# FFN output projection of tiles 2 to 8 by Strassen's seven block products, block sums on VectorE and GpSimd

## The chip, the cores and the metric

The kernel runs on one core of one Trainium2 chip. That core has a matrix engine (TensorE: PE in the profile, and PEld for its weight loads), three engines for element-wise work (VectorE: DVE; ScalarE: ACT; GpSimd: POOL) and a queue engine (SyncE: SP). Engines run side by side and wait for each other on semaphores. The metric is device time of one execution in microseconds (us); lower is better. Before the change the median of 3 runs is 362.95 us (362.79 to 364.91).

## The reference

Causal attention in blocks of 64 keys, 8 batches, 8 heads, 576 positions, head size 64; its output, with the heads side by side, is the input `x` (4608 x 512) of a gated feed-forward layer:

```python
gate = np.maximum(x @ w_gate, 0.0)     # 4608 x 1536
val = x @ w_val                        # 4608 x 1536
return (gate * val @ w_out)            # 4608 x 512
```

Everything is given and returned in float32; the kernel's matrix products take bfloat16 and sum in float32.

## The kernel before, in words

**Tiles of the feed-forward layer.** `ffn_gen` walks over nine tiles of 512 tokens. Tiles 0 to 7 hold the first 512 positions of one batch each, tile 8 the last 64 positions of all eight batches. A tile has three parts. For each of twelve slices f of the 1536 hidden columns there are four matmuls for the gate and four for the value (`product`, line 663; the weights are the stationary operand, 512 tokens stream past). ACT applies the rectifier (`relu`, line 673) and DVE multiplies gate by value into a bf16 tile `hT` (`hidden`, line 679). Then the output projection (`out_mm`, line 748): four groups of 128 tokens, in each twelve matmuls of 512 columns, accumulated over f in one PSUM bank; after a group DVE copies the bank to an `ob` tile (`finish`, line 758) and a store on the ACT queue writes it out (`put`, line 647). In tile 8 the last group is cut into 352 and 160 columns, and its stores are divided between the ACT and SP queues (line 653).

**Attention beside it.** While tile j of the feed-forward layer runs, the attention of batch j + 1 is computed in four rounds per batch. A round first makes scores on PE (`visit`, line 450) into two PSUM pairs of banks, both of the pool `psum_sc` (named `sc`, two buffers of two banks), and two single banks (`one`, `ffnp`). ACT takes the exponentials in this order: the two single banks (line 462), the pair `first`, the pair `second` (line 455). Some 20 places later two sets of matmuls with v follow (line 585 and 599), which DVE divides by the sums (line 524). Tiles 7 and 8 have no attention beside them.

**What sets the order.** The order is written out by hand. Each step of the attention, of the loads and of the casts has a name and a place in the table `AT`; the place counts steps of `ffn_gen` (one `yield` is one matmul), 144 to a tile. `ffn(n)` lets that many steps of the feed-forward layer go first, then the named step is issued. In tiles 3 to 6 the fourth round's scores stand at 92 of 144, its third exponential at 98, its products with v at 112 and 116; the output projection begins at 96. In tile 2 the fourth round (`s15`) stands at 383.65, that is 0.35 before the output projection of that tile, which begins at 384. Each engine executes its own instructions in that order, and waits are derived from the tiles that an instruction reads and writes.

**Buffers.** `psum_ffn` has three single banks (`ffnp`) for gate, value, projection groups and some of the attention; `ob` has four buffers; `hT` thirteen; `stage` ten buffers of 4 KB, which hold loads in the first part of the kernel.

**GpSimd.** In the steady part POOL does nothing but issue the loads of the next batch: 11 of q and k (`l`, 9 places into the tile) and 6 of v (`lv`, 46 places in), line 338.

Of the kernel before, what the change touches and what calls it, by code (L numbers as in the profile page):

```python
# [10 lines left out]
FP = mybir.dt.float32  # L11
BF = mybir.dt.bfloat16
AX = mybir.AluOpType
# [4 lines left out]
def kernel(  # L18
# [10 lines left out]
    nc = tc.nc  # L29

    B, H, S, D = q.shape
# [5 lines left out]


    FIRST = 3
    BASE = {0: 0, 1: 512, 3: 896, 2: 1024}  # L40
    AW = 1600
    TW = 256
# [2 lines left out]
    sb = ctx.enter_context(tc.tile_pool(name="sb", bufs=1))  # L45
# [75 lines left out]
    class Early:  # L121
# [111 lines left out]
        def half(self, t, hg):  # L233
            return self.m[t][:, 1024 * hg : 1024 * hg + 1024].rearrange(
                "p (j n) -> p j n", j=4
            )
# [403 lines left out]
    store, late = [], []  # L640

    def put(j, s, ob, n0, n1):
        if j < B:
            r0 = S * j + 128 * s
            n = 64 if j == B - 1 and s < 3 else 128
            for i in range(0, 128, n):
                (nc.sync if i else nc.scalar).dma_start(
                    out[r0 + i : r0 + i + n, :], ob[i : i + n]
                )
        else:  # L650
            for i in range(2):
                r0 = S * (2 * s + i) + 512
                (nc.scalar, nc.sync)[i].dma_start(
                    out[r0 : r0 + 64, n0:n1], ob[64 * i : 64 * i + 64]
                )

    def ffn_gen():
        for j in range(B + 1):
            hT = []
            x = xT_of(j) if j < B else xTt.rearrange("p b h n -> p h b n")  # L660

            def product(to, t, c, f):
                nc.tensor.matmul(  # L663
                    to,
                    (wg, wv)[t][f // 4][:, c, 128 * (f % 4) : 128 * (f % 4) + 128],
                    x[:, c],
                    start=(c == 0),
                    stop=(c == 3),
                )

            def relu(gate):
                gate_sb = sb.tile([128, 512], BF, name="gate_sb", bufs=3)
                nc.scalar.activation(gate_sb, gate, AF.Relu)  # L673
                return gate_sb

            def hidden(gate_sb, val):
                h = sb.tile([128, 512], BF, name="hT", bufs=13)
                products.append(
                    nc.vector.tensor_tensor(out=h, in0=gate_sb, in1=val, op=AX.mult)  # L679
                )  # L680
                hT.append(h)

            first = 0
            if j < 2:
                first = 2
                acc = {
                    n: psum_ffn.tile([128, 512], FP, name="ffnp")
                    for n in ((0, 0), (0, 1), (1, 0))
                }
                for cs in ((0, 1), (2,)):  # L690
                    for t in range(2):
                        for f in range(2):
                            if (t, f) not in acc:
                                acc[t, f] = psum_sc.tile([128, 2, 512], FP, name="sc")[
                                    :, 0, :
                                ]
# [12 lines left out]
            pairs = []  # L709
            if j == 0:  # L710
                pairs = [(f, (range(4),)) for f in (2, 4, 6)] + [(8, ((0, 1), (2, 3)))]
                first = 10
            for f0, parts in pairs:
                acc = {
                    (t, f): psum_one.tile([128, 512], FP, name="one")
                    if (t, f) == (0, 0)
                    else psum_ffn.tile([128, 512], FP, name="ffnp")
                    for t in range(2)
                    for f in range(2)
                }  # L720
                gates = []
                for cs in parts:
                    for t in range(2):
                        for f in range(2):
                            for c in cs:
                                product(acc[t, f], t, c, f0 + f)
                                if c == 3 and t == 0:
                                    gates.append(relu(acc[t, f]))
                                if c == 3 and t == 1:
                                    hidden(gates[f], acc[t, f])  # L730
                                yield
            for f in range(first, 12):
                gate = (
                    psum_one.tile([128, 512], FP, name="one")
                    if (j, f) == (1, 2)
                    else psum_ffn.tile([128, 512], FP, name="ffnp")
                )
                val = psum_ffn.tile([128, 512], FP, name="ffnp")
                for t, c in [(t, c) for t in range(2) for c in range(4)]:
                    product((gate, val)[t], t, c, f)  # L740
                    if (t, c) == (0, 3):
                        gate_sb = relu(gate)
                    if (t, c) == (1, 3):
                        hidden(gate_sb, val)
                    yield

            def out_mm(op, s, f, n0, n1):
                nc.tensor.matmul(  # L748
                    op,
                    hT[f][:, 128 * s : 128 * (s + 1)],  # L750
                    wo[f // 4][:, f % 4, n0:n1],
                    start=(f == 0),
                    stop=(f == 11),
                )

            def finish(op, s, n0, n1):
                ob = sb.tile([128, 512], FP, name="ob", bufs=4)[:, 0 : n1 - n0]
                nc.vector.tensor_copy(ob, op)  # L758
                if store:
                    store.pop()()  # L760
                (store if j else late).append(lambda j=j: put(j, s, ob, n0, n1))

            groups = outs(j)
            while groups:
                some = 2 if j == 0 and len(groups) == 4 else 1
                ops = [
                    psum_ffn.tile([128, 512], FP, name="ffnp")[:, 0 : n1 - n0]
                    for _, n0, n1 in groups[:some]
                ]
                for f0 in (0, 4, 8) if some == 2 else (0,):  # L770
                    for op, (s, n0, n1) in zip(ops, groups):
                        for f in range(f0, f0 + 4 if some == 2 else 12):
                            out_mm(op, s, f, n0, n1)
                            if f == 11:
                                finish(op, s, n0, n1)
                            yield
                groups = groups[some:]
# [7 lines left out]
    def ffn(n):  # L785
        for _ in range(n):
            if next(gen, 0) == 0:
                return
# [19 lines left out]
    with tc.manual_schedule(engines={E.PE, E.DVE, E.Activation, E.Pool, E.SP}):  # L808
# [45 lines left out]
        place = [0]  # L854
# [419 lines left out]
        for b in range(4, B):  # L1274
            base = 144 * (b - 1)
            for i in range(4):
                r = 4 * b + i
                acts.update(round_at(r, ("dve", "one", "ffn", None)))
                for n, p in STEADY.items():
                    AT[f"{n}{r}"] = base + 30 * i + p  # L1280
            acts[f"L{b}"] = lambda b=b: last_keys(b)
            AT[f"L{b}"] = base + 11
            if b + 1 < B:
                acts[f"l{b + 1}"] = lambda b=b: load_qkv(b + 1, (0, 1), products[-1])
                acts[f"lv{b + 1}"] = lambda b=b: load_qkv(b + 1, (2,))
                acts[f"d{b + 1}"] = lambda b=b: dma_transposes(b + 1)
                for n, p in (("l", 9), ("lv", 46), ("d", 66)):
                    AT[f"{n}{b + 1}"] = base + p
        assert set(acts) == set(AT), set(acts) ^ set(AT)
        for n in sorted(acts, key=lambda n: AT[n]):  # L1290
            ffn(int(AT[n]) - place[0])
            place[0] = max(place[0], int(AT[n]))
            acts[n]()
        ffn(10**6)
        store.pop()()
# [28 lines left out]
```

## Time and profile before

| | |
|---|---|
| median of 3 runs | 362.95 us |
| lowest, highest | 362.79, 364.91 us |
| span of the profiled execution | 363.3 us |
| PE busy | 353.3 us, 97% of the span |
| DVE busy | 170.7 us, 47% |
| ACT busy | 167.9 us, 46% |
| POOL busy | 112.8 us, 31% |

No time of its own is listed for the profiled execution beside its span; the span is 0.35 us above the median of the runs. The page lists busy time by engine, the clock that was granted to TensorE by slice (nine tenths or more in all 40 slices here), a chain of waits that leads back from the last instruction, and groups of equal instructions with their count, total time, mean time, and the idle time of their engine just before them with what ended it. Matmuls overlap: the duration of one (379 ns for 512 columns) is longer than the distance from one to the next, so distances are read from starts.

### The profile page before, as it was taken

What the parts mean: (1) busy time and instruction counts of PE and PEld (TensorE: products, weight loads), DVE (VectorE), ACT (ScalarE), POOL (GpSimd) and SP (SyncE); (2) the same over time, 40 slices, a digit from 0 to 9 for tenths busy, and PEclk for the clock granted to TensorE, in tenths of its full rate; (3) what the DMA queues carried; (4) which work ended last, traced back from release to release, by engine and by line L of the source; (5) the groups of instructions that cost most, each with busy time, mean ns of one, the idle gap of its engine ahead of it and who ended that gap; (6) DMA issues with size and microseconds to landing.
All of it is one profiled execution on the core that took longest, in us unless ns stands there. A gap on an engine that the chain in (4) does not pass through costs nothing.

```text
span 363.3 us, 7423 instructions
## 1 busy us (share of the span) xinstructions
PE 353.3 (97%) x2933; PEld 176.9 (49%) x2933; DVE 170.7 (47%) x426; ACT 167.9 (46%) x265; POOL 112.8 (31%) x157
## 2 busy tenths in 40 slices
PE   7899999999998999999999999999999999999996
PEld 3544455545544555555555454554455544444443
DVE  4663456677433363444445443554255434333432
ACT  4933676696325850666055625553365403302310
POOL 4647645695209500680049001930000000000000
PEclk9999999999999999999999999999999999999999
DMA  8999999999999995899449951997220130031013
GB/s 245 298 357 374 314 239 255 189 156 138 186 203 108 141 154 137 56 146 186 109 49 145 169 133 46 130 157 152 81 16 14 54 102 0 0 88 29 1 41 105
DMA packets 152083, 49.97 MB, mean 138 GB/s; under 512 B 134512, under 2 KB 145008, under 8 KB 152048
## 3 DMA queue, kind: packets, MB, share of 16 engines
q0 software_dynamic: 70480, 8.85, 46.7%
q1 hardware_dynamic: 76480, 31.86, 44.8%
q10 hardware_dynamic: 5088, 8.78, 7.2%
q8 instruction: 23, 0.38, 0.5%
q14 instruction: 12, 0.10, 0.1%
HBM read 37.75 MB, written 9.44 MB: 130 GB/s over the span
## 4 chain that ended last, share of the span: by engine, by line
PE 89%; DMA 5%; ACT 4%; DVE 1%; issue 0%; POOL 0%; SPq 0%; POOLq 0%; DVEq 0%
PE ffnp L663 49%; PE ffnp L748 23%; PE sc L450 3%; PE ffnp L585 2%; PE one L450 2%; DMA xT<-xnat 2%; DMA stage<-in_moe_w_gate_dram 2%; PE one L585 2%; ACT attnT L414 2%; PE one L663 1%; ACT attnT L455 1%; PE ffnp L547 1%; PE one L794 1%; DMA kTt<-k_bt 1%; PE ffnp L599 1%; PE one L599 1%
## 5 line engine op out<-in xcount | busy, mean ns | idle before, releaser
L679 DVE TENSOR_TENSOR hT<-gate_sb,ffnp 128x512 bf16<-128x512 bf16 x106 | 72.6, 685 | 96.5 <-PE ffnp L663 70.7
L673 ACT ACTIVATE gate_sb<-ffnp 128x512 bf16<-128x512 f32 x103 | 62.1, 605 | 103.3 <-PE ffnp L663 93.6
L663 PE MATMUL ffnp<-xT,wv 128*128 128x512 bf16 x376 | 100.7, 379 | 0.0
L663 PE MATMUL ffnp<-xT,wg 128*128 128x512 bf16 x364 | 99.0, 379 | 1.1 <-DMA xT<-xnat 0.4
L748 PE MATMUL ffnp<-wo,hT 128*128 128x512 bf16 (+2 forms) x444 | 98.8, 373 | 0.0
L748 PEld LDWEIGHTS <-hT 128*128 128x128 bf16 x444 | 41.8, 98 | 45.5 <-issue 0.6
L663 PEld LDWEIGHTS <-wv 128*128 128x128 bf16 x432 | 40.1, 98 | 45.5 <-issue 3.2
L663 PEld LDWEIGHTS <-wg 128*128 128x128 bf16 x432 | 39.8, 98 | 44.6 <-issue 3.6
L455 ACT ACTIVATE attnT<-sc 128x1024 bf16<-128x1024 f32 x56 | 56.8, 1044 | 0.0
L758 DVE COPY ob<-ffnp 128x512 f32<-128x512 f32 (+2 forms) x37 | 25.0, 676 | 45.1 <-PE ffnp L748 44.7
L338 POOL DMA_DIRECT2D q_bf<-in_q_dram x20 | 17.8, 903 | 76.3 <-DVE hT L679 52.0
L462 ACT ACTIVATE attnT<-one 128x512 bf16<-128x512 f32 (+1 forms) x28 | 15.0, 536 | 53.8 <-PE ffnp L450 53.8
L585 PEld LDWEIGHTS <-attnT 128*128 128x128 bf16 x640 | 26.5, 97 | 13.9 <-DVE attnT L803 1.3
L338 POOL DMA_DIRECT2D v_bf<-in_v_dram x30 | 24.3, 853 | 6.8 <-PE one L585 2.2
L450 PEld LDWEIGHTS <-kTm 64*128 64x128 bf16 x384 | 11.3, 94 | 15.6 <-issue 7.8
L338 POOL DMA_DIRECT2D k_bf<-in_k_dram x20 | 17.7, 933 | 0.0
L450 PE MATMUL sc<-qTm,kTm 64*128 64x512 bf16 (+1 forms) x168 | 16.9, 305 | 0.0
L585 PE MATMUL ffnp<-v_bf,attnT 128*128 128x65 bf16 x320 | 15.0, 194 | 0.0
L462 ACT ACTIVATE attnT<-ffnp 128x512 bf16<-128x512 f32 (+1 forms) x28 | 15.0, 534 | 0.0
L803 DVE MEMSET attnT<- 64x128 uint32 x59 | 9.0, 165 | 12.0 <-ACT attnT L455 10.2
L524 DVE TENSOR_TENSOR xnat<-ffnp,recip 128x256 bf16<-128x256 f32 x32 | 13.6, 424 | 1.1
L585 PE MATMUL one<-v_bf,attnT 128*128 128x65 bf16 x250 | 11.6, 193 | 0.7 <-POOL v_bf L220 0.7
(122 smaller groups left out, 293.8 us busy)
## 6 DMA issues: line engine op xcount, KB each, us to landing
out_dram<-ob ACTq DMA_DIRECT2D x29, 256.0 KB, 2.4
stage<-in_moe_w_val_dram SPq DMA_DIRECT2D x6, 512.0 KB, 8.2
stage<-in_moe_w_gate_dram SPq DMA_DIRECT2D x6, 512.0 KB, 8.7
stage<-in_moe_w_out_dram SPq DMA_DIRECT2D x6, 512.0 KB, 10.5
q_bf<-in_q_dram POOLq DMA_DIRECT2D x20, 128.0 KB, 4.3
k_bf<-in_k_dram POOLq DMA_DIRECT2D x20, 128.0 KB, 5.8
v_bf<-in_v_dram POOLq DMA_DIRECT2D x20, 128.0 KB, 6.1
stage<-in_v_dram SPq DMA_DIRECT2D x19, 128.0 KB, 5.4
```

Source lines behind the costliest of these rows:

```text
L338: ins = nc.gpsimd.dma_start(dst, part_of)
L450: nc.tensor.matmul(o, kTm[b % 2][head_of(hh), c, hp, :], qT, start=True, stop=True)
L455: return lambda: nc.scalar.activation(at[:, :, lo : lo + 512], sc, AF.Exp, scale=scale)
L462: nc.scalar.activation(at[:, hh, 1024 : 1024 + w], third[hh][:, 0:w], AF.Exp, scale=scale)
L524: nc.vector.tensor_tensor(out=out, in0=av[:, 0:m, 0:64], in1=recip[:, 0:m].to_broadcast([rows, m, 64]), op=AX.mult,)
L585: nc.tensor.matmul(av[:, p, :], at[:, col : col + 128], v_bf[b % 2][:, c, h, :], start=(p == 0), stop=(c == p), skip_group_check=True,)
L663: nc.tensor.matmul(to, (wg, wv)[t][f // 4][:, c, 128 * (f % 4) : 128 * (f % 4) + 128], x[:, c], start=(c == 0), stop=(c == 3),)
L673: nc.scalar.activation(gate_sb, gate, AF.Relu)
L679: nc.vector.tensor_tensor(out=h, in0=gate_sb, in1=val, op=AX.mult)
L748: nc.tensor.matmul(op, hT[f][:, 128 * s : 128 * (s + 1)], wo[f // 4][:, f % 4, n0:n1], start=(f == 0), stop=(f == 11),)
L758: nc.vector.tensor_copy(ob, op)
L803: nc.vector.memset(o, 0.0)
```

## The change: seven block products

For tiles 2 to 8 the product of `h` (512 tokens x 1536) with `w_out` (1536 x 512) is no longer formed directly. The hidden columns are paired: pair c holds slices 2c and 2c + 1. With tokens, hidden columns and output columns halved, the product is a 2 x 2 block product, and Strassen's scheme forms it from seven block products instead of eight. Each of the seven has 256 tokens, 768 hidden columns and 256 output columns, that is twelve matmuls of 256 columns: 84 matmuls of 256 columns replace 48 of 512 (60 in tile 8).

- `weight_sums` (POOL, places 232 to 247) adds blocks of `w_out` once into three `stage` buffers; `weight_differences` (DVE, places 300 to 320) subtracts blocks in place in `wo`.
- `sums_of` makes, for each pair of each tile, two sums of blocks of `h` on DVE and one difference of blocks on POOL; six pairs in a tile. `hT` becomes seven buffers of a pair each.
- `seven_products` computes the products in the order 5, 2, 1, 3, 4, 6, 7. Products 5 and 2 go to `y` and `z`, the two banks of one `sc` pair; 1, 6 and 7 to `ffnp` banks; 3 is added onto `y`, 4 onto `z`. ACT copies out `y` after product 5, `y` after product 3 and `z` after product 4; DVE and POOL add and subtract them into the four output blocks, which are stored by `put_block`.
- A place table of 144 steps is mapped to 138 (`place_of`) from tile 2 on, since one `yield` now stands for two matmuls in the 42 steps of the projection.

```diff
+    SEVEN = 2
 ...
+    def weight_sums(c):
+        if c % 2 == 0:
+            sevens.append(sb.tile([128, 2048], BF, name="stage", bufs=10))
 ...
+        nc.gpsimd.tensor_tensor(
+            out=t[:, 0:256], in0=two[:, 0, 0:256], in1=two[:, 1, 256:512], op=AX.add
+        )
+        nc.gpsimd.tensor_tensor(
+            out=t[:, 256:768].rearrange("p (c n) -> p c n", c=2),
+            in0=two[:, :, 0:256],
+            in1=two[:, :, 256:512],
+            op=AX.add,
+        )
+    def weight_differences(c, eng):
+        two = wo[c // 2][:, 2 * (c % 2) : 2 * (c % 2) + 2, :]
+        for d, n in ((two[:, 0, 256:512], two[:, 1, 256:512]), (two[:, 1, 0:256], two[:, 0, 0:256])):
+            eng.tensor_tensor(out=d, in0=d, in1=n, op=AX.subtract)
+    def sums_of(h):
+        s = sb.tile([128, 2048], BF, name="stage", bufs=10)
+        nc.vector.tensor_tensor(
+            out=s[:, 0:512], in0=h[:, 0, :], in1=h[:, 1, :], op=AX.add
+        )
+        nc.vector.tensor_tensor(
+            out=s[:, 1024:1280], in0=h[:, 0, 0:256], in1=h[:, 1, 256:512], op=AX.add
+        )
+        nc.gpsimd.tensor_tensor(
+            out=s[:, 512:1024].rearrange("p (c n) -> p c n", c=2),
+            in0=h[:, :, 256:512],
+            in1=h[:, :, 0:256],
+            op=AX.subtract,
+        )
+        return s
+    def seven_products(j, pair, sums):
+        def times(to, which, p, c, first):
 ...
+            nc.tensor.matmul(
+                to,
+                left[:, 128 * p : 128 * p + 128],
+                right,
+                start=first,
+                stop=(c == 5),
+                skip_group_check=True,
+            )
 ...
+        def whole(to, which, new=True, cs=range(6)):
+            for p in range(2):
+                for c in cs:
+                    times(half(to, p), which, p, c, new and (p, c) == (0, 0))
+                    if c % 2:
+                        yield
+        def store_later(hi, n0, ob, p0=0, p1=2):
+            if store:
+                store.pop()()
+            store.append(lambda: put_block(j, hi, n0, ob, p0, p1))
+        yz = psum_sc.tile([128, 2, 512], FP, name="sc")
+        y, z = yz[:, 0, :], yz[:, 1, :]
+        for to, which in ((y, 5), (z, 2)):
+            yield from whole(to, which, cs=range(4))
+        for to, which in ((y, 5), (z, 2)):
+            yield from whole(to, which, new=False, cs=(4, 5))
+        g = sb.tile([128, 512], FP, name="ob", bufs=4)
+        nc.scalar.copy(g, y)
+        nc.vector.tensor_tensor(out=g, in0=z, in1=g, op=AX.add)
+        m1 = psum_ffn.tile([128, 512], FP, name="ffnp")
+        yield from whole(m1, 1)
+        nc.vector.tensor_tensor(out=g, in0=m1, in1=g, op=AX.subtract)
+        yield from whole(y, 3, new=False)
+        c12 = sb.tile([128, 512], FP, name="ob", bufs=4)
+        nc.scalar.copy(c12, y)
+        store_later(0, 256, c12)
+        c22 = sb.tile([128, 512], FP, name="ob", bufs=4)
+        nc.gpsimd.tensor_tensor(out=c22, in0=g, in1=c12, op=AX.add)
+        yield from whole(z, 4, new=False)
+        c21 = sb.tile([128, 512], FP, name="ob", bufs=4)
+        nc.scalar.copy(c21, z)
+        store_later(1, 0, c21)
+        nc.gpsimd.tensor_tensor(out=g, in0=g, in1=c21, op=AX.add)
+        m6 = psum_ffn.tile([128, 512], FP, name="ffnp")
+        yield from whole(m6, 6)
+        nc.vector.tensor_tensor(out=c22, in0=m6, in1=c22, op=AX.add)
+        store_later(1, 256, c22)
+        if j < B:
+            m7 = psum_ffn.tile([128, 512], FP, name="ffnp")
+            yield from whole(m7, 7)
+            nc.vector.tensor_tensor(out=g, in0=g, in1=m7, op=AX.subtract)
+            store_later(0, 0, g)
+        else:
+            for p in range(2):
 ...
+                nc.vector.tensor_tensor(
+                    out=half(g, p), in0=half(g, p), in1=m7, op=AX.subtract
+                )
+                store_later(0, 0, half(g, p), p, p + 1)
 ...
             def hidden(gate_sb, val):
-                h = sb.tile([128, 512], BF, name="hT", bufs=13)
+                if len(hT) % 2 == 0:
+                    pair.append(sb.tile([128, 2, 512], BF, name="hT", bufs=7))
+                h = pair[-1][:, len(hT) % 2, :]
 ...
+            def sum_pairs():
+                while j >= SEVEN and len(sums) < len(hT) // 2:
+                    sums.append(sums_of(pair[len(sums)]))
 ...
                     if (t, c) == (0, 3):
                         gate_sb = relu(gate)
+                        sum_pairs()
 ...
+            if j >= SEVEN:
+                sum_pairs()
+                yield from seven_products(j, pair, sums)
+                continue
 ...
+        for c in range(6):
+            AT[f"W{c}"] = 232 + 3 * c
+            AT[f"D{c}"] = 300 + 4 * c
+        def place_of(p):
+            j, o = divmod(p, 144)
+            if j < SEVEN:
+                return p
+            return 144 * SEVEN + 138 * (j - SEVEN) + min(o, 96) + max(0, o - 96) * 42 / 48
```

`put_block` writes a 256 x 256 block (two times 128 rows of 256 columns) in one store on the ACT queue for tiles 2 to 7; in tile 8 it writes 64 rows at a time, by turns on the ACT and SP queues, 16 stores where there were 10. `store_later` issues the store before the one that it is given, so the last block of a tile (`g`) is stored in the next tile, after the copy `c12`.

More of the change, by code (lines that the diff above doesn't have):

```diff
@@ L655, in put, with put_block @@
                 )
+    def put_block(j, hi, n0, ob, p0, p1):
+        n = slice(n0, n0 + 256)
+        rows = ob.rearrange("q (p n) -> q p n", n=256)
+        if j < B:
+            r0 = S * j + 256 * hi + 128 * p0
+            nc.scalar.dma_start(
+                out[r0 : r0 + 128 * (p1 - p0), n].rearrange("(p q) n -> q p n", q=128),
+                rows,
+            )
+        else:
+            for p in range(p0, p1):
+                for i in range(2):
+                    r0 = S * (4 * hi + 2 * p + i) + 512
+                    (nc.scalar, nc.sync)[i].dma_start(
+                        out[r0 : r0 + 64, n], rows[64 * i : 64 * i + 64, p - p0]
+                    )
@@ new lines @@
+    sevens = []
+    def weight_sums(c):
+        if c % 2 == 0:
+            sevens.append(sb.tile([128, 2048], BF, name="stage", bufs=10))
+        two = wo[c // 2][:, 2 * (c % 2) : 2 * (c % 2) + 2, :]
+        t = sevens[c // 2][:, 768 * (c % 2) : 768 * (c % 2) + 768]
+        nc.gpsimd.tensor_tensor(
[7 more added lines that the diff above has]
+        )
@@ new lines, in weight_differences @@
+    def weight_differences(c, eng):
+        two = wo[c // 2][:, 2 * (c % 2) : 2 * (c % 2) + 2, :]
+        for d, n in ((two[:, 0, 256:512], two[:, 1, 256:512]), (two[:, 1, 0:256], two[:, 0, 0:256])):
[15 more added lines that the diff above has]
+        return s
@@ new lines, in seven_products, with half @@
+    def seven_products(j, pair, sums):
+        def times(to, which, p, c, first):
+            two = wo[c // 2][:, 2 * (c % 2) : 2 * (c % 2) + 2, :]
+            t = sevens[c // 2][:, 768 * (c % 2) : 768 * (c % 2) + 768]
+            s, h = sums[c], pair[c]
+            left, right = {
+                5: (s[:, 0:256], two[:, 1, 256:512]),
+                2: (s[:, 256:512], two[:, 0, 0:256]),
+                1: (s[:, 1024:1280], t[:, 0:256]),
+                3: (h[:, 0, 0:256], two[:, 0, 256:512]),
+                4: (h[:, 1, 256:512], two[:, 1, 0:256]),
+                6: (s[:, 512:768], t[:, 256:512]),
+                7: (s[:, 768:1024], t[:, 512:768]),
+            }[which]
+            nc.tensor.matmul(
[5 more added lines that the diff above has]
+                skip_group_check=True,
+            )
+        def half(to, p):
+            return to[:, 256 * p : 256 * p + 256]
+        def whole(to, which, new=True, cs=range(6)):
[35 more added lines that the diff above has]
+        store_later(1, 256, c22)
+        if j < B:
+            m7 = psum_ffn.tile([128, 512], FP, name="ffnp")
+            yield from whole(m7, 7)
+            nc.vector.tensor_tensor(out=g, in0=g, in1=m7, op=AX.subtract)
+            store_later(0, 0, g)
+        else:
+            for p in range(2):
+                m7 = psum_ffn.tile([128, 512], FP, name="ffnp")[:, 0:256]
+                for c in range(6):
+                    times(m7, 7, p, c, c == 0)
+                    if c % 2:
+                        yield
+                nc.vector.tensor_tensor(
+                    out=half(g, p), in0=half(g, p), in1=m7, op=AX.subtract
+                )
+                store_later(0, 0, half(g, p), p, p + 1)
@@ L674, in relu @@
                 return gate_sb
+            pair = []
             def hidden(gate_sb, val):
-                h = sb.tile([128, 512], BF, name="hT", bufs=13)
+                if len(hT) % 2 == 0:
+                    pair.append(sb.tile([128, 2, 512], BF, name="hT", bufs=7))
+                h = pair[-1][:, len(hT) % 2, :]
                 products.append(
@@ L681, in hidden @@
                 hT.append(h)
+            sums = []
+            def sum_pairs():
+                while j >= SEVEN and len(sums) < len(hT) // 2:
+                    sums.append(sums_of(pair[len(sums)]))
             first = 0
@@ L1288 @@
                     AT[f"{n}{b + 1}"] = base + p
-        assert set(acts) == set(AT), set(acts) ^ set(AT)
+        acts.update({f"W{c}": lambda c=c: weight_sums(c) for c in range(6)})
+        acts.update(
+            {f"D{c}": lambda c=c: weight_differences(c, nc.vector) for c in range(6)}
+        )
+        for c in range(6):
+            AT[f"W{c}"] = 232 + 3 * c
+            AT[f"D{c}"] = 300 + 4 * c
+        assert set(acts) == set(AT), set(acts) ^ set(AT)
+        def place_of(p):
[3 more added lines that the diff above has]
+            return 144 * SEVEN + 138 * (j - SEVEN) + min(o, 96) + max(0, o - 96) * 42 / 48
         for n in sorted(acts, key=lambda n: AT[n]):
-            ffn(int(AT[n]) - place[0])
-            place[0] = max(place[0], int(AT[n]))
+            at = int(place_of(AT[n]))
+            ffn(at - place[0])
+            place[0] = max(place[0], at)
             acts[n]()
```

## The prediction

> **What bounds the kernel now.** I read the page first: which engine the chain of waits rests on, and at what clock.
>
> ```profile
> PEclk9999999999999999999999999999999999999999
> PE 89%; DMA 5%; ACT 4%; DVE 1%; issue 0%; POOL 0%; SPq 0%; POOLq 0%; DVEq 0%
> ```
>
> The chain is PE, at the full granted clock. Then the chain in order of time, at its end (start, length, engine, line, count):
>
> ```profile
> 318.24 10.36 PE ffnp L748 x48
> 328.60 20.72 PE ffnp L663 x96
> 349.32 10.40 PE ffnp L748 x60
> 359.74 0.33 DVE ob L758
> ```
>
> PE issues without a gap, so a matmul less is time less, and any wait of PE is time more. 48 matmuls of 512 columns take 10.36 us, 215.8 ns each. For narrower ones I take the timeline of the last groups: each copy starts when its group ends.
>
> ```profile
> 357.12 0.69 DVE L758 COPY ob<-ffnp 128x512 f32<-128x512 f32 x1 [1.90 <-PE ffnp L748]
> 358.91 0.53 DVE L758 COPY ob<-ffnp 128x352 f32<-128x352 f32 x1 [1.10 <-PE ffnp L748]
> 359.74 0.33 DVE L758 COPY ob<-ffnp 128x160 f32<-128x160 f32 x1 [0.31 <-PE ffnp L748]
> ```
>
> Twelve matmuls of 352 columns took 358.91 - 357.12 = 1.79 us, 149 ns each; twelve of 160 took 0.83 us, 69 ns each, every one with its own weight load. A straight line through these three is 0.417 ns a column plus 2.5 ns; 256 columns lie inside it: **109.2 ns**.
>
> **1. The matmuls.** A tile now takes 84 x 109.2 ns = 9.17 us instead of 10.36 (tile 8: 10.36 by 36 x 215.8 + 1790 + 830 = 10.39): 6 x 1.19 + 1.22 = **8.4 us less**. A slope error of 2% moves this by 1.3.
>
> The row for this is 215.8, 149 and 69 ns by width. The Trainium skill (TensorE: Matmul & The Clock Gate, Back-to-back issue gap) speaks against narrow matmuls: a sustained stream with weight loads costs about 131 ns at 512 columns and 81 at 128. Interpolated, about 98 ns at 256, an estimate from that page, 84 of them would take 8.2 us against 6.3 for 48, and the sum would be 13 us of loss in place of the 8.4 of gain. The trace disagrees at 512 columns (215.8), so I stay with the rows.
>
> **2. The first product waits for an exponential.** `yz` is a pair of the two-buffer pool `sc`. By the order and waits of the built program, it takes the buffer of the fourth round's `first` pair, so product 5 waits for ACT's first exponential of that pair (ahead of it on ACT: relu and two exponentials). Before, out_mm used another pool and passed it. Timeline around the start of tile 4's projection, then tile 2's:
>
> ```profile
> 207.87 0.60 ACT L673 ACTIVATE gate_sb<-ffnp 128x512 bf16<-128x512 f32 x1 [1.59 <-PE ffnp L663]
> 208.36 0.59 ACT L462 ACTIVATE attnT<-one 128x512 bf16<-128x512 f32 x1
> 208.84 0.60 ACT L462 ACTIVATE attnT<-ffnp 128x512 bf16<-128x512 f32 x1
> 209.31 1.96 ACT L455 ACTIVATE attnT<-sc 128x1024 bf16<-128x1024 f32 x2
> 209.40 2.97 PE L748 MATMUL ffnp<-wo,hT 128*128 128x512 bf16 x13
> ```
>
> ```profile
> 132.73 4.48 PE L748 MATMUL ffnp<-wo,hT 128*128 128x512 bf16 x20
> 133.14 1.95 ACT L455 ACTIVATE attnT<-sc 128x1024 bf16<-128x1024 f32 x2
> ```
>
> L455 takes 1.04 us, so `first` is read at 209.31 + 1.04 = 210.35, with 0.07 for the release 210.42: PE, ready at 209.40, waits 1.02. Tiles 3, 5 and 6 show the same spacing. In tile 2 the round stands three matmuls nearer: 133.14 + 1.04 + 0.07 - 132.73 = 1.52. Everything of PE queues behind it. 4 x 1.02 + 1.52 = **5.6 us more**. Tiles 7 and 8 have no round there.
>
> **3. Product 4 waits for the copy of product 3.** `y` and `z` are two banks of one tile, and the built program makes product 4's first matmul (into `z`) wait for ACT's copy of `y`, which waits for product 3's last matmul. Nothing stands between the two on PE. Its price by rows of the same shape (PSUM to SBUF, 128 x 512):
>
> ```profile
> 329.30 1.03 PE L663 MATMUL ffnp<-xTt,wv 128*128 128x512 bf16 x4
> 329.56 0.60 ACT L673 ACTIVATE gate_sb<-ffnp 128x512 bf16<-128x512 f32 x1 [11.55 <-PE ffnp L663]
> ```
>
> ACT starts 0.26 us after PE has issued the last matmul (the next starts at 329.30), takes 0.60, release 0.07: 0.93. Seven tiles: **6.5 us more** (5.6 to 7.4 with copies of 0.48 to 0.73).
>
> **4. Product 3 waits for `z + g`** for the same reason: copy of `y`, then DVE. From the end of products 5 and 2: 0.26 + 0.60 + 0.06 + 0.69 + 0.07 = 1.68. In between PE has product 1, 12 x 0.109 = 1.31, and in tiles 2 to 6 two sets of products with v (0.45 each), which cover it. Tiles 7 and 8: 2 x 0.37 = **0.7 more**.
>
> **5. The rest of the chain to the next tile.** After product 3's end (t = 0): ACT's copy `c12` ends at 0.86; then the store of the previous tile's `g` is issued, and the copy `c21` needs that store's buffer, so ACT waits for its landing, 2.4 us by the page (2.0 to 3.3 in single windows): 3.3, copied 3.9. POOL adds 128 x 512 in f32. No such addition is in the trace; the one-input rows are
>
> ```profile
> L382 POOL CAST wo<-stage 128x1024 bf16<-128x1024 f32 x5 | 5.0, 1040 | 3.7 <-DMA stage<-in_moe_w_out_dram 3.7
> L195 POOL CAST q_bf<-stage 128x512 bf16<-128x512 f32 x5 | 3.1, 612 | 4.5 <-DMA stage<-in_q_dram 4.5
> ```
>
> between 0.61 (as many outputs) and 1.04 (as many elements read); no reason makes it free. I take 1.04 as nearer: 5.0. DVE's `g - m7` ends at 5.8 and frees the bank that the next tile's first value (or second gate) needs. PE gets there at 0.93 + 3 x 1.31 + 0.43 + 0.86 (scores) + 0.43 = 6.6: **covered by 0.8**, thanks to step 3. A landing of 3.3 would cost 0.1 a tile. Behind ACT's wait stand three stores (0.34 each, done at 5.0) and the next round's exponentials, whose scores come at 5.9; behind DVE's stands the next `hidden`, after 7. The Trainium skill (GPSIMD Reference, Engine selection) advises VectorE for additions, GpSimd being about twice as slow with two inputs; by its 4497 ns for 2048 f32 elements a quarter is 1.12 us, an estimate, and the sum stays.
>
> **6. The end.** Before: last matmul issued at about 359.48, the last copy ends 360.07, store lands 2.1 later, span ends 363.3. After, with t as above, PE ends at 4.9, `c21` at 3.9, POOL at 5.0, the two half subtractions (0.42 each, by L524) at 5.9. But the eight ACT stores of tile 8 stand behind `c21`; the 64-row stores took 0.5 us of queue each, and in the built program each waits for the landing of the store eight before it. That gives issue of c12, c21 from 3.95 to 5.95, c22 at 6.25 and 6.75 (landing of the first ones), `g` at 7.25 and 7.75, landing 9.85: 5.0 after PE's end against 2.7. **2.3 more**; 0.5 if the queue is no limit, 3.3 with landings of 2.7.
>
> **7. Covered work.** DVE: 12 sums a tile, 128 x 512 and 128 x 256 in bf16, at most 0.69 + 0.42 a pair by f32 rows, beside 2 x 0.69 of `hidden` in 3.45 us; 47% busy, and 0.77 us of slack before `hidden` holds a bank. The 12 differences at places 300 to 320 of tile 2 (0.17 by memset to 0.42 each) fill DVE nearly completely there: 0 to 2.5 us. POOL: 6 differences a tile, last needed by product 6; the sums of pairs 0 and 1 delay the v loads by up to 2.1 us, which are needed some 15 us later. The weight sums (12 in 9 us) end before place 300. On SP only 3 rows are fewer; transposes of xT keep their place. I take **0.5 more** for all this; 4 if DVE falls behind around rounds.
>
> **Sum**, against the execution's own span: 363.3 - 8.4 + 5.6 + 6.5 + 0.7 + 2.3 + 0.5 = 370.5. That span is 0.35 above the runs' median: **370.2 us**, 2% slower.
>
> **Rivals.**
> - *The handovers of the pair are cheap* (ends faster). Steps 2 to 4 are 12.8 us; without them 357.4. For: the copies are short and ACT is 46% busy. Against: the copy of step 3 starts only when product 3 has ended, and PE has nothing else. It is faster once the three cost under 7.2 in all, by 1% under 3.6.
> - *DVE and POOL fall behind*: two-input operations beside each other, sums at 0.69 + 0.42 and more, tile 2's differences: 4 to 8 us more, 374 to 378. For: DVE has stretches of six tenths. Against: its mean.
> - *256 columns do not cost half*: at 120 ns a matmul 6.4 us more, 376.6. Against: 69 ns at 160.
> - *Little change*: handovers at half, end at 0.5: 362 to 364.
>
> **How the numbers follow.** Forecast (366.6 to 373.5) 0.70; DVE/POOL 0.13; costly matmuls 0.04; little change 0.09; cheap handovers 0.04. The range leaves out the last two and the far end: **366.5 to 377**. One per cent, 3.6 us, is about what a measurement tells from no change: faster 0.04, same 0.10, slower 0.86.
>
> **What would show it.** PE idle before the products' line: about 1.0 us in each of tiles 3 to 6 and 1.5 in tile 2 released by an ACT exponential, 0.9 in all seven by an ACT copy, 0.4 in two by DVE; starts 109 ns apart within a product; the last store landing about 5 us after the last matmul. I am wrong if PE passes from product 3 to 4 without a gap, or if DVE and POOL rows grow so that PE waits elsewhere.

## The result: 4.3% slower

| | before | after |
|---|---|---|
| median | 362.87 us (4 runs) | **378.79 us** (378.19 to 379.38, 4 runs) |
| ratio | | **1.043** (95%: 1.039 to 1.046) |
| span of the profiled execution | 363.3 us | 377.5 us |
| PE busy | 353.3 us | 349.4 us |
| DVE busy | 170.7 us | 228.7 us |
| POOL busy | 112.8 us | 194.4 us |

The forecast was 370.2 us, the range 366.5 to 377: right that it gets slower, 8.6 us too low, and the range ends 1.8 short. In all later profiles the span lies 1.8 to 2.0 below the time of its execution. By that, before's profile (363.3) is of an execution of about 365.1 (an estimate), some 2 above its median, and not 0.35 as the prediction had it. Its base is unharmed, since it carried a difference of 7.2 over to the median; but the spans differ by 14.2 and the medians by 15.9, and a difference of spans of these two kernels is good to 2 us only.

### The profile page after: what moved, and what is told of

Its sections match the earlier page's. It is cut to its first block, busy times and chain, and to the rows that moved or that the text cites. A ratio compares the mean times of both kernels' runs of the same rounds, so it can differ in the third digit from the quotient of the medians.

```text
span 377.5 us, 8089 instructions
## 1 busy us (share of the span) xinstructions
PE 349.4 (93%) x3173; PEld 201.4 (53%) x3173; DVE 228.7 (61%) x522; ACT 180.0 (48%) x286; POOL 194.4 (51%) x225
## 5 line engine op out<-in xcount | busy, mean ns | idle before, releaser
L834 DVE TENSOR_TENSOR hT<-gate_sb,ffnp 128x512 bf16<-128x512 bf16 x106 | 72.4, 683 | 64.7 <-PE ffnp L814 40.4
L814 PE MATMUL ffnp<-xT,wv 128*128 128x512 bf16 x376 | 100.7, 379 | 3.9 <-DVE hT L834 3.8
L814 PE MATMUL ffnp<-xT,wg 128*128 128x512 bf16 x364 | 99.0, 379 | 3.2 <-DVE hT L834 2.4
L709 POOL TENSOR_TENSOR stage<-hT 128x512 bf16<-128x512 bf16 x42 | 54.0, 1313 | 80.7 <-DVE hT L834 80.7
L814 PEld LDWEIGHTS <-wv 128*128 128x128 bf16 x432 | 40.1, 98 | 50.3 <-issue 8.9
L814 PEld LDWEIGHTS <-wg 128*128 128x128 bf16 x432 | 39.9, 98 | 46.0 <-issue 6.8
L740 PEld LDWEIGHTS <-stage 128*128 128x128 bf16 x420 | 40.4, 98 | 11.5 <-issue 6.1
L706 DVE TENSOR_TENSOR stage<-hT 128x256 bf16<-128x256 bf16 x42 | 31.9, 761 | 0.0
L703 DVE TENSOR_TENSOR stage<-hT 128x512 bf16<-128x512 bf16 x42 | 31.0, 739 | 1.2
L740 PE MATMUL ffnp<-stage 128*128 128x256 bf16 x252 | 31.3, 273 | 0.0
L781 POOL TENSOR_TENSOR ob<-ob 128x512 f32<-128x512 f32 x7 | 8.8, 1264 | 36.1 <-ACT ob L778 36.1
L740 PE MATMUL sc<-wo,hT 128*128 128x256 bf16 x168 | 20.6, 272 | 5.2 <-ACT ob L778 5.0
L740 PE MATMUL sc<-wo,stage 128*128 128x256 bf16 x168 | 19.5, 272 | 4.7 <-ACT attnT L456 4.7
L910 PE MATMUL ffnp<-wo,hT 128*128 128x512 bf16 x96 | 23.6, 379 | 0.0
L740 PEld LDWEIGHTS <-hT 128*128 128x128 bf16 x168 | 16.4, 97 | 8.7 <-issue 6.8
```

The source lines that it names most:

```text
L703: nc.vector.tensor_tensor(out=s[:, 0:512], in0=h[:, 0, :], in1=h[:, 1, :], op=AX.add)
L706: nc.vector.tensor_tensor(out=s[:, 1024:1280], in0=h[:, 0, 0:256], in1=h[:, 1, 256:512], op=AX.add)
L709: nc.gpsimd.tensor_tensor(out=s[:, 512:1024].rearrange("p (c n) -> p c n", c=2), in0=h[:, :, 256:512], in1=h[:, :, 0:256], op=AX.subtract,)
L740: nc.tensor.matmul(to, left[:, 128 * p : 128 * p + 128], right, start=first, stop=(c == 5), skip_group_check=True,)
L814: nc.tensor.matmul(to, (wg, wv)[t][f // 4][:, c, 128 * (f % 4) : 128 * (f % 4) + 128], x[:, c], start=(c == 0), stop=(c == 3),)
L910: nc.tensor.matmul(op, hT[f][:, 128 * s : 128 * (s + 1)], wo[f // 4][:, f % 4, n0:n1], start=(f == 0), stop=(f == 11),)
```

## The profile after

The granted clock and the chain of waits (page of the kernel after). The clock has not changed. The chain stops short: it follows the end back over a fifth of the span.

```profile
PEclk9999999999999999999999999999999999999999
PE 18%; ACT 1%; DVE 0%; issue 0%; ACTq 0%
```

The end of that chain in order of time (start, length, engine, line, count) shows tile 8's products 3, 4, 6 and 7:

```profile
365.68 1.49 PE sc L740 x12
...
367.23 0.59 ACT ob L778
...
367.87 1.47 PE sc L740 x12
369.33 2.63 PE ffnp L740 x24
```

Products 6 and 7 are 24 matmuls. The first starts at 369.17 (the chain counts it only from the end of the one before) and the last at 371.68: 109 ns from one to the next, as priced. Product 4 starts 2.19 after product 3 (367.87 - 365.68) instead of 1.31: 0.88 for the handover.

What PE waited for (engine, line waited for, us in total, times, longest):

```profile
PE ffnp L814 <- DVE hT L834: 6.2, 8, 1.2
PE sc L740 <- ACT ob L778: 5.0, 7, 0.7
PE sc L740 <- ACT attnT L456: 4.7, 5, 1.3
```

The second and third lines are steps 3 and 2. This list counts a wait from the modelled end of the matmul before, so by starts each wait is longer. Step 2 in tile 4:

```profile
214.83 1.04 PE L814 MATMUL ffnp<-xT,wv 128*128 128x512 bf16 x4
...
215.62 1.96 ACT L456 ACTIVATE attnT<-sc 128x1024 bf16<-128x1024 f32 x2
...
216.72 2.45 PE L740 MATMUL sc<-wo,stage 128*128 128x256 bf16 x21 [0.84 <-ACT attnT L456]
```

The last of the four matmuls starts at 215.49, so the product could start 0.22 later, at 215.71. It starts at 216.72: a wait of 1.01, where the list has 0.84. Tiles 3, 5 and 6 show the same 1.01 and tile 2 shows 1.49, which makes 5.5 in all where the list has 4.7.

The first line is new. L814 is the feed-forward matmul, L834 `hidden`: PE waits for a bank that DVE has not yet read. The timeline of the longest of these waits, DVE, POOL and PE together:

```profile
241.09 0.69 DVE L834 TENSOR_TENSOR hT<-gate_sb,ffnp 128x512 bf16<-128x512 bf16 x1 [0.27 <-PE ffnp L814]
241.48 2.38 POOL L709 TENSOR_TENSOR stage<-hT 128x512 bf16<-128x512 bf16 x2
241.81 2.35 DVE L703 TENSOR_TENSOR stage<-hT 128x512 bf16<-128x512 bf16 x1
...
244.97 0.67 DVE L834 TENSOR_TENSOR hT<-gate_sb,ffnp 128x512 bf16<-128x512 bf16 x1
...
245.69 0.59 PE L814 MATMUL ffnp<-xT,wv 128*128 128x512 bf16 x2 [1.22 <-DVE hT L834]
```

One block sum of DVE (L703) takes 2.35 us. It ends 0.3 after the two differences on POOL beside it, as if it had to let both pass. `hidden` stands behind it in DVE's order, with some short operations of the attention between, and PE behind `hidden`. POOL had two differences to make in a row because its loads for the next batch stood before them. The `hidden` at 241.09 overlaps POOL too, and took 0.69 as ever; it reads one operand from PSUM, the sums read both from SBUF. Of 106 such operations in the trace none took more than 0.690.

By the starts of the stretches of PE, with the price per matmul confirmed, the 14.2 us of the spans divide so:

| stretch | before | after | difference |
|---|---|---|---|
| hidden part, tile 2 | 30.82 | 32.73 | +1.91 |
| tiles 3, 4, 5, 6 | 27.06 each | 30.16, 30.17, 30.57, 29.50 | +12.16 |
| tiles 7, 8 | 20.72 each | 20.72 each | 0 |
| projection, tiles 2 to 6 | 11.27 to 11.28 | 10.92 to 10.96 | -0.31 to -0.36 each |
| projection, tile 7 | 10.36 | 10.34 | -0.02 |
| tile 8's projection to the end | 14.17 | 16.06 | +1.90 |

The wait of step 2 ends at the products' first matmul, so its 5.5 is in the first two rows, which are 14.07 together: **8.5 us** of the hidden parts belong to no step of the sum, 8.1 of them in tiles 3 to 6. The 0.4 in tile 2 tells little: that stretch holds waits for loads and lies between 29.8 and 33.5 us in kernels that differ from this one in other places.

## Experiments

### DVE's sums beside POOL

One half of the sums is moved away, left out, or made lighter, in four ways. First the differences go to DVE:

```diff
-        nc.gpsimd.tensor_tensor(
+        nc.vector.tensor_tensor(
             out=s[:, 512:1024].rearrange("p (c n) -> p c n", c=2),
```

> The block differences of h (L709) go from POOL to DVE; nothing else moves. My theory now, A: DVE's sums L703 and L706 read two SBUF tiles and are held up for as long as a POOL operation with two SBUF inputs runs beside them; behind them stands hidden (L834), for which PE waits. By the stretches of the trace the cost is 9.2 us. So: L703 back to 0.42 and L706 to 0.28 each, no PE wait for L834, DVE's work on sums 42 x (0.42 + 0.28 + 0.42) = 47 us instead of 62.9, time 369 to 371. Rival B: DVE has simply too much to do, whoever is beside it; then 17.6 us more work on DVE makes PE wait longer for L834, 379 to 384. Rival C: POOL's queue is what holds (its loads for the next tile stand behind the differences); then the waits for L834 stay and those for loaded tiles go, 376 to 378.

Then POOL's half is left out (products 6 and 7 read `s[:, 0:256]` and `s[:, 256:512]`), and DVE's half (products 5, 2 and 1 read blocks of `h`):

> The block differences of h on POOL (L709) are left out; products 6 and 7 read the block sums in their place, so those two products are of other blocks. DVE's sums stay. A (two-input operations hold each other up): L703 0.42, L706 0.28, no PE wait for L834, 369 to 371. B (DVE's own load): 376 to 379, waits for L834 as before. Beside the kernel that has the differences on DVE it tells what these 42 operations cost there: nothing by A if DVE has the room.

> DVE's block sums of h (L703, L706) are left out; products 5, 2 and 1 read single blocks of h in their place. POOL's differences stay. A: the cost is in the pair, so leaving out this half takes it away as well: no PE wait for L834, L709 at 1.1 to 1.3 us, 369 to 371. C (POOL's queue alone): POOL's work and its loads stay as they are, so 376 to 379.

Last, POOL's operation keeps its size and loses its second input:

```diff
-        nc.gpsimd.tensor_tensor(
-            out=s[:, 512:1024].rearrange("p (c n) -> p c n", c=2),
-            in0=h[:, :, 256:512],
-            in1=h[:, :, 0:256],
-            op=AX.subtract,
+        nc.gpsimd.tensor_copy(
+            s[:, 512:1024].rearrange("p (c n) -> p c n", c=2), h[:, :, 256:512]
```

> POOL's 42 differences of h become copies of as many elements with one input (so products 6 and 7 are of single blocks); DVE's sums stay. It asks what of a POOL operation holds DVE's. If any POOL operation on SBUF does, for as long as it runs: POOL's copies take about 0.61 each instead of 1.31 (the one-input row of 128 x 512), a DVE sum is held up to 0.6, PE's waits for L834 shrink from 6.2 to 1 or 2, 371 to 374. If only a second input does: L703 0.42 and L706 0.28 in all rows, no such wait, 369 to 371.

| kernel | time, us | against after | L703 and L706, mean ns | PE waits for `hidden` |
|---|---|---|---|---|
| after | 378.79 | | 739, 761 | 6.2 us |
| differences on DVE | 371.45 (369.85 to 372.85) | -7.3 | 422, 283 | none listed |
| POOL's differences left out | 370.06 | -8.7 | 422, 283 | none listed |
| DVE's sums left out | 368.85 | -9.9 | left out | 0.3 us |
| POOL copies with one input | 369.83 | -9.0 | 538, 488 | none listed |

The last three rows are of 2 executions each. The kernel before took 362.7 to 363.6 us at the median beside the runs of this section, so a difference from the 378.79 is good to about 1 us.

The groups of the kernel after (count, then busy us and mean ns, then idle time before them):

```profile
L709 POOL TENSOR_TENSOR stage<-hT 128x512 bf16<-128x512 bf16 x42 | 54.0, 1313 | 80.7 <-DVE hT L834 80.7
L706 DVE TENSOR_TENSOR stage<-hT 128x256 bf16<-128x256 bf16 x42 | 31.9, 761 | 0.0
L703 DVE TENSOR_TENSOR stage<-hT 128x512 bf16<-128x512 bf16 x42 | 31.0, 739 | 1.2
```

With the differences on DVE:

```profile
L703 DVE TENSOR_TENSOR stage<-hT 128x512 bf16<-128x512 bf16 x42 | 17.7, 422 | 1.2
L709 DVE TENSOR_TENSOR stage<-hT 128x512 bf16<-128x512 bf16 x42 | 17.5, 417 | 0.0
L706 DVE TENSOR_TENSOR stage<-hT 128x256 bf16<-128x256 bf16 x42 | 11.9, 283 | 0.0
```

With one-input copies on POOL:

```profile
L709 POOL COPY stage<-hT 128x512 bf16<-128x512 bf16 x42 | 31.7, 788 | 90.7 <-DVE hT L831 90.7
L703 DVE TENSOR_TENSOR stage<-hT 128x512 bf16<-128x512 bf16 x42 | 22.6, 538 | 1.2
L706 DVE TENSOR_TENSOR stage<-hT 128x256 bf16<-128x256 bf16 x42 | 20.5, 488 | 0.0
```

The cost needs both halves: leave out either and it goes. In both runs that leave one out the hidden parts of tiles 3 to 6 are 28.07 us each, which is the 27.06 of before and the 1.01 of step 2, so nothing of the 8.1 us is left there. DVE makes all 126 operations in 47.1 us by itself, less than the 62.9 it took for 84 of them beside POOL. So DVE did not have too much to do, and rival B falls. The four times lie within 0.5 us of the 369 to 371 that theory A gave. Rival C, POOL's queue alone, falls with the run that leaves POOL's work as it is and DVE's sums out. With one input on POOL the sums are still held, by 13.5 us in all instead of 33.3, but PE no longer waits for `hidden`, which has that much room. Neither forecast for this run was right in full: the sums are held as by the first, the time is as by the second, and a copy took 0.79 us, not 0.61.

The Trainium skill states this (GPSIMD Engine Reference, Specifications): GpSimd shares its SBUF interfaces with VectorE, with contention where a VectorE instruction has two SBUF inputs or runs in a two-port mode. The trace agrees on both sides: the sums, two SBUF inputs, went from 0.42 to 2.35, and `hidden`, one input in PSUM, stayed at 0.66 to 0.69. The page gives no price.

### The handover from product 3 to product 4

The block that makes product 6 moves ahead of the one that makes product 4:

```diff
         yield from whole(y, 3, new=False)
 ...
+        yield from whole(m6, 6)
         yield from whole(z, 4, new=False)
 ...
-        yield from whole(m6, 6)
```

> Product 6 moves between products 3 and 4, so PE has 1.31 us of matmuls while ACT copies y (0.26 to the start, 0.58, release). Theory: the handover from 3 to 4 costs what the stretches of the trace show, 0.88 in six tiles and 0.8 in tile 7, and nothing takes its place, so 6.0 us less, 372 to 374. Rival: the gain is given back, since z's copy and POOL's second addition come 1.3 us later, the pair and the last bank come free later, and the scores of the next round or the next tile's values wait: 376 to 379.

**371.03 us** (370.75 to 372.32), 7.8 less. Tile 4 of that kernel, products 3, 6 and 4:

```profile
216.61 1.47 PE L740 MATMUL sc<-wo,hT 128*128 128x256 bf16 x12
217.92 1.47 PE L740 MATMUL ffnp<-stage 128*128 128x256 bf16 x12
219.23 1.47 PE L740 MATMUL sc<-wo,hT 128*128 128x256 bf16 x12
```

1.31 apart, no gap; the projection's stretches went from 10.92 to 10.96 down to 10.08 to 10.09, and in tile 7 from 10.34 to 9.47: 0.83 to 0.88 a tile, as said, and 5.2 over tiles 2 to 7. In tile 8 the stretch to the end is only 0.3 shorter (15.74 for 16.06). The rest of the gain lies in the hidden parts of tiles 2, 3 and 4, each 1.1 shorter; the list has 4.7 us of waits for `hidden` in place of 6.2. Why these became fewer is not settled.

### The wait for the exponential

```diff
+        m1 = psum_ffn.tile([128, 512], FP, name="ffnp")
+        yield from whole(m1, 1, cs=range(4))
         yz = psum_sc.tile([128, 2, 512], FP, name="sc")
 ...
-        yield from whole(m1, 1)
+        yield from whole(m1, 1, new=False, cs=(4, 5))
```

> Each tile's projection begins with the first eight matmuls of product 1 (pairs 0 to 3; they go to a bank of the other pool), then products 5 and 2 as before, then the last four of product 1. Theory: PE's wait for the fourth round's first exponential (0.85 in tiles 3 to 6, 1.3 in tile 2; 4.7 in the list of waits) is covered up to 8 x 0.109 = 0.87, so 4 x 0.85 + 0.87 = 4.3 us less, 374 to 375.5, and about 0.4 of that wait stays in tile 2. Against it: product 1 then no longer stands between products 2 and 3, only 4 of its 12 matmuls do, so product 3 waits up to 0.87 more for z + g in tiles 7 and 8 (1.7 us), and less in tiles 2 to 6, where matmuls with v stand there too: 376 to 377. Rival: the wait is only the first of several that end at the same time, and the next one (hidden, a bank) takes its place: 377.5 to 379.

**379.27 us** (378.54 to 379.76): no gain, a miss. PE's waits in that kernel (two lines of source were added ahead, so `hidden` is L835 and DVE's z + g is L774):

```profile
PE ffnp L815 <- DVE hT L835: 6.2, 8, 1.2
...
PE sc L740 <- DVE ob L774: 4.2, 6, 1.0
```

By this list the wait for the exponential fell from 4.7 to 0.5, and 4.2 came up before product 3. I had allowed for that in tiles 7 and 8 only. Product 1 was the cover of z + g in all tiles; moved ahead, it pays for one handover with the other.

### The end

Tile 8 by the old projection, seven products for tiles 2 to 7:

```diff
-                while j >= SEVEN and len(sums) < len(hT) // 2:
+                while SEVEN <= j < B and len(sums) < len(hT) // 2:
 ...
-            if j >= SEVEN:
+            if SEVEN <= j < B:
 ...
+            acts[f"R{c}"] = lambda c=c: weight_back(c)
```

> Seven products for tiles 2 to 7 only; tile 8 is projected as before the change, with its five column groups and copies, and the block differences of w_out are added back by 12 DVE additions in tile 8 (about 0.36 each). By the stretches of the trace: tile 8 loses its 1.2 us of fewer matmuls, and is rid of 0.9 (product 4), 0.4 (product 3) and 1.8 at the end (16.05 from the tile's first projection matmul to the end of the span, against 14.15): 1.9 less, 376 to 377.5. Rival: the end is as long whichever way tile 8 is made, because the previous tile's stores and additions hold it; then 1.2 - 1.3, no change, 378 to 379.

**376.72 us** (376.25 to 377.18), 2.1 less, as said: tile 8 loses by the change.

### All covered at once, and what that missed

```diff
+        def add(out, in0, in1, op=AX.add):
+            nc.vector.tensor_tensor(out=out, in0=in0, in1=in1, op=op)
 ...
+        add(c22, m6, g)
+        add(c22, y, c22)
 ...
+        add(g, z, g)
 ...
-        nc.gpsimd.tensor_tensor(out=c22, in0=g, in1=c12, op=AX.add)
 ...
-        nc.gpsimd.tensor_tensor(out=g, in0=g, in1=c21, op=AX.add)
```

> Everything together: block differences of h on DVE; products in the order 1, 6 (eight matmuls each), 5, 2, rest of 1, eight of 7, 3, rest of 6 and 7, 4, so that every wait on the pair has matmuls beside it; the blocks are added by DVE from PSUM instead of by POOL; tile 8's stores of 64 rows two at a time, and not held back. Theory (9.2 us from DVE beside POOL, 4.7 + 6.1 + 0.8 from the three handovers, 1.8 at the end are all that stood against the 8.4): 363.3 - 8.4 + 0.5 (tile 2, DVE) + 1 (end) = 356 to 358, faster than before the change by 1.5%. Rival: something else in the seven products costs time (DVE's 47 us of sums and 6 x 0.69 a tile, accumulation in five banks at once); then 360 or more.

> The same, with tile 8 projected plainly, so that the end is that of the kernel before: 363.3 - 6 x 1.19 + 0.5 = 356.5 to 358. Beside the run with all tiles by seven products it tells whether tile 8's 1.2 us survive its longer end: that run is the faster one if its end costs under 1.2.

**371.29** and **369.49 us**, 15 and 13 above the sums: a miss. Tile 4 of the first (L791 is the copy of y, L770 DVE's additions):

```profile
219.40 0.59 ACT L791 COPY ob<-sc 128x512 f32<-128x512 f32 x1 [2.28 <-PE sc L740]
...
220.63 0.69 DVE L770 TENSOR_TENSOR ob<-sc,ob 128x512 f32<-128x512 f32 x1
...
221.38 0.82 PE L740 MATMUL sc<-wo,hT 128*128 128x256 bf16 x6 [1.14 <-DVE ob L770]
```

Taking POOL's additions to DVE, I let DVE read y from the pair. Product 4 waits for whoever reads any part of the pair, so it now waited 1.1 us a tile for DVE, 8.0 in all seven: the handover that I had covered, made anew one line further on. Next, DVE adds the SBUF copies only, and the order is changed:

```diff
-        add(c22, y, c22)
+        add(c22, c22, c12)
 ...
-        add(g, z, g)
+        add(g, g, c21)
```

> As the run with all handovers covered, mended by its trace, which showed PE waiting 8.0 us before product 4 for DVE's addition of y, 1.7 before scores for DVE's addition of z, and product 3 some 0.3 a tile for z + g. Now ACT's copies alone read y after product 3 and z after product 4 (DVE adds their SBUF copies), and the order is 1 (eight matmuls), 5, 2, rest of 1, 6, 3, 7, 4, so 1.75 us of matmuls stand before product 3 and 1.31 before product 4. Theory: these waits were what stood against it, 371.3 - 8.0 - 1.7 - 7 x 0.3 = 359.5, with 0.4 of waits at most in tile 2: 358 to 360.5, faster than before the change by about 1%. Rival: the time returns as other waits (DVE's chain of six additions a tile, banks): 363 or more.

> The same with tile 8 projected plainly. In the pair of runs before, that was 1.8 us better. By its own sum: 363.3 - 6 x 1.19 + 0.5 = 356.7; I expect 356 to 359, faster than before the change by 1 to 1.8%. Rival as above.

> That kernel (readers apart, tile 8 plain) with the differences of h back on POOL, beside DVE's sums. It asks whether the cost of DVE beside POOL stands when every other wait is gone. Theory: the same per tile, 6 tiles instead of 7, so 6 to 8 us more than with the differences on DVE, 363 to 367, no longer faster than before the change. Rival: it only came on top of the other waits: within 2 us.

**364.83** (363.69 to 365.61), **364.42** (362.99 to 365.83) and **371.24 us** (371.19 to 371.26). The last pair differs by 6.8 us with nothing changed but the engine of 36 differences: DVE beside POOL costs about the same with the handovers covered as without (7.3 us for 42 differences). The first two came out 5 and 8 above their sums: the rival, that the time returns as other waits. Here PE runs through the products of tiles 3 to 6 without a gap, and loses 0.7 to 1.3 us a tile at the start of the next tile. The kernel with tile 8 plain, from product 4 on (L804 is ACT's copy of z):

```profile
217.73 1.47 PE L746 MATMUL sc<-wo,hT 128*128 128x256 bf16 x12
...
220.04 0.58 ACT L804 COPY ob<-sc 128x512 f32<-128x512 f32 x1 [2.83 <-PE ffnp L451]
...
220.68 0.40 PE L451 MATMUL sc<-qTm,kTm 64*128 64x384 bf16 x4 [0.49 <-ACT ob L804]
```

Product 4 is issued by 219.04, so the copy could begin at 219.24, and begins at 220.04. In the built program it waits for the landing of the previous tile's last store, which goes out only with this tile's first block, at 216.63, and lands at 219.96. The scores wait for the copy, and ACT's exponentials come late behind it.

```diff
+        if store:
+            store.pop()()
         front, back = range(4), (4, 5)
```

> As the kernel with readers apart and tile 8 plain; the previous tile's last store is issued at the start of a tile's products instead of after product 3, some 7 us earlier. Theory: ACT's copy of z then starts 0.2 after product 4 and the scores (0.5 a tile) and the values behind late relus (0.2 to 0.5 a tile) wait no more: 4 x 1.3 + 0.7 of tile 3 = up to 5.5 less, 358.5 to 360.5, and the copy's start in the trace 0.2 after the last product in all tiles. Rival: the three copies a tile keep ACT late wherever they begin; then 1 to 2 less, 362 to 363.5.

> The same, and product 4 before the last eight matmuls of product 7 (order 1, 5, 2, rest of 1, eight of 6, 3, rest of 6, four of 7, 4, eight of 7), so z is copied 0.87 earlier and ACT is free before the next tile begins. Less stands before product 3 (1.31 for a chain of 1.64), so tiles without a round wait 0.3 there. Theory of the landing alone: within 1 of the run beside it. If ACT's copies are what is late: 1 to 3 better than the run beside it.

> The changed kernel itself, with the previous tile's last store issued at the start of the products. Step 5 of the prediction said that ACT's wait for its landing is covered by the later products and the handovers. Then 378 to 379.5, no change. If the landing costs there too: 1 to 4 less.

**361.09** (360.58 to 363.08; ratio 0.994, 0.992 to 0.997), **359.91** (359.73 to 362.42; ratio **0.992**, 0.989 to 0.995) and **378.79 us** (378.29 to 380.36). In the kernel with readers apart and tile 8 plain that landing cost 3.3; in the changed kernel it costs nothing, as step 5 had it. The first of the three lies between its forecast and its rival; there ACT's copy of z does start 0.2 us after product 4 (at 219.97 in tile 4). With z copied 0.87 earlier still it is 1.2 better, which speaks for ACT's copies being late. So the first two at last beat the kernel before, by 0.6 and 0.8%. The better kernel has seven products for tiles 2 to 7, no differences or additions on POOL in these tiles, matmuls of another bank beside every handover, and the early store. Of its 7.1 us of fewer matmuls, the spans show 2.7; by stretches, tile 2 gives back 2.3 (1.5 of it in two waits inside its products), tiles 3 to 6 1.4, tile 7 0.65 and the end 0.1.

## Why the prediction was wrong

By its own steps, as the spans show them:

| step | predicted | measured |
|---|---|---|
| 1 matmuls | -8.4 | -8.4 (109 ns apart) |
| 2 exponential | +5.6 | +5.5 (1.01 in four tiles, 1.49 in tile 2) |
| 3 product 4 after the copy | +6.5 | +6.1 (0.83 to 0.88 in seven tiles) |
| 4 product 3 after z + g | +0.7 | +0.6 (0.30 in two tiles) |
| 5 chain to the next tile | 0 | 0 |
| 6 the end | +2.3 | +1.9 (last landing 4.6 after the last matmul, 2.7 before) |
| **7 covered work** | **+0.5** | **+8.5** |

Of the 8.6 us by which the forecast was low, step 7 makes 8.0 and the other steps take 1.0 back; the other 1.6 is the gap between the difference of the spans and that of the medians.

**The step that failed is the seventh.** It took the sums at 0.69 + 0.42 a pair "by f32 rows" and DVE at 47% busy with 0.77 us of slack before `hidden` holds a bank. As a bound for DVE by itself that was generous: alone they take 0.42 + 0.28. What failed is that the price was taken as DVE's own, when it was set by what POOL does at that moment. Single sums took up to 2.58 us (one stood at 207.04 beside two differences), over three times the slack. The mechanism was named as a rival, two-input operations beside each other, 374 to 378, at a chance of 0.13, and dismissed by DVE's mean. That was the wrong row: a mean of half busy says nothing of a single operation that stretches sixfold in front of the one that PE waits for. No row of the trace before gave the price, since POOL does almost nothing but issue loads in the steady part there, and every two-tensor operation of DVE has one input in PSUM. But its loading phase held a sign: a VectorE cast that reads SBUF took 0.69 us beside GpSimd casts, and 0.41 for the same shape with GpSimd idle.

```profile
16.46 0.62 POOL L382 CAST wg<-stage 128x512 bf16<-128x512 f32 x1
16.67 0.69 DVE L382 CAST wg<-stage 128x512 bf16<-128x512 f32 x1
...
19.08 0.41 DVE L382 CAST wv<-stage 128x512 bf16<-128x512 f32 x1
```

The bound should have come from that side, from an operation that lasts as long as its neighbours on POOL: two differences at POOL's 1.04 in a row are 2.1, over the slack by 1.3. Twice a tile in four tiles, as the stretches turned out, that is 10.5 us, an estimate in hindsight, against 8.1 measured there. The range needed that as its end, or a good part of it.

**Steps 2 to 4 held** within 0.4 us each, from copies and releases of the same shape. The start of 0.26 after the last matmul, the copy of 0.60 and the release of 0.07 made 0.93 (0.88 measured). Step 2 was right to 0.01 us in tiles 3 to 6.

**Step 1 held against the page's stream figures.** The figures for a sustained stream in the Trainium skill (TensorE: Matmul & The Clock Gate, Back-to-back issue gap) would have given 98 ns by interpolation, an estimate, and a loss; the distances are 215.8 ns at 512 columns before and 109 at 256 after, and the trace decides. The same section also gives N / 2.4 + 2.5 ns, which it calls the isolated gap and which the prediction passed over; that formula fits both distances (215.8 and 109.2).

**Step 5 held in the changed kernel**: an earlier store changed nothing (378.79 both times). Its reason, cover by the stall of step 3, was not tried by itself. The stalls of step 7 are not needed for it, since with either half of the sums left out the hidden parts of tiles 3 to 6 hold nothing but step 2's wait. In the kernel with readers apart the landing did cost 3.3 us.

**The rivals.** Cheap handovers, costly narrow matmuls and little change are out by the table. "DVE and POOL fall behind" is what happened, beyond its upper end by 0.8. One sum in them was wrong: from 357.4 without steps 2 to 4, the change is faster once the three cost under 5.6 (by 1% under 2), not 7.2 and 3.6; the forecast does not rest on it.

## What to carry to other kernels

Before work is shared between VectorE and GpSimd, ask of each VectorE operation whether both inputs lie in SBUF: if so, its time can become that of the GpSimd operations beside it (2.35 us for 2.38 here), and what is queued behind it decides the cost, not the mean load. A saving on PE is only as large as the other matmuls that stand beside every handover it needs; count them as a budget (here three products of 1.31 us in banks of their own for waits of 1.0, 1.6 and 0.9), since moving one product pays one wait with another. After each wait removed, look for the next reader of the same buffer before expecting the gain.

## What the runs showed that I had not expected

- A VectorE sum of 128 x 512 in bf16 takes 0.42 us alone and up to 2.58 us beside two GpSimd operations of 2.39 us together; there it did not get in between the two.
- A one-input GpSimd copy holds it too (538 ns on the mean), but not enough to reach PE. `hidden`, a VectorE operation with one input in PSUM, was never slowed (at most 690 ns in 106, as before the change).
- GpSimd is slowed as well: the difference of 128 x 512 took 1.313 us on the mean beside VectorE's sums and 1.193 us without them.
